# Attention with exponentials on two engines: the third shift of some VectorE tiles made by an accumulating transfer

## The chip, the cores and the metric

The kernel runs on one core of a Trainium2 chip. Times are device microseconds (us). The engines are TensorE (PE: matmuls, and PEld: its weight loads), VectorE (DVE), ScalarE (ACT), GpSimd (POOL) and SyncE (SP, which here only issues transfers). Each has its own queue of instructions and works through it in order. They meet through semaphores. Sixteen DMA engines move the data of every transfer.

## The reference

The program computes attention for 32 heads of 2048 queries and keys, with head size 20. Rows of q and k are scaled to length one, and a head has one factor t in place of the usual scale.

```python
qn = q / (jnp.sqrt((q * q).sum(axis=-1, keepdims=True)) + eps)
kn = k / (jnp.sqrt((k * k).sum(axis=-1, keepdims=True)) + eps)
logits = jnp.einsum('bhqd,bhkd->bhqk', qn, kn) * t[None, :, None, None]
attn = _softmax(logits, axis=-1)
return jnp.einsum('bhqk,bhkd->bhqd', attn, v)
```

All tensors are bf16. The dominant work is 32 x 2048 x 2048 exponentials.

## The kernel before, in words

**Tiles.** Keys lie on the 128 partitions, sixteen blocks of 128 (R = 16) in each head, and the 2048 queries in four groups of 512 columns. A tile is one block of keys by all queries: 128 x 2048 scores. The list `DVE_TILES` says how many of a head's sixteen tiles DVE works on; the others are ACT's, cut into units of 512 columns.

**ACT's tiles.** PE computes two or three units of scores into one of two halves of psA ("wave", line 758), ACT takes the exponential of all of them in one instruction into `p_ring` (line 849), and PE multiplies four units with V into psO (line 778). V has a column of ones, so that the same product sums the softmax's denominator.

**DVE's tiles.** PE computes scores into psD. DVE multiplies them and adds a constant, with an int16 result in a slot of `xt` (line 905, two conversions of 1024 columns to a tile, tasks `t1`). Read as fp16, that integer is a rough exponential. To flatten its error, the kernel averages four of them: the integer itself and three copies, shifted by 256, 512 and 768 (`PHASES`), each multiplied with V scaled by the matching power of two (`vph`, made on POOL, line 574). The shifts are integer additions from `xt` into `ss` (line 912 on DVE, tasks `s0`, `s1`, `s2`). The planner can give a shift to POOL instead, cut into pieces of 128 to 672 int32 words, each fitted into the time of a conversion on DVE (line 916). So a DVE tile costs two conversions, three shifts and four groups of products with V. There are `NX` = 6 slots of `xt` and `NE` = 4 of each `ss`.

**Preparation.** q, k and v are loaded by SP some three heads ahead (`LEAD`). DVE squares and sums, and computes the inverse root in a few small operations (tasks `rs`, lines 623 to 641); POOL folds the squares and normalizes (lines 612, 653). SP transposes, and copies q into a zero-padded layout `qz` and k into three rotated copies `kR`. Head 0 is prepared in its own way, with a scratch tensor `kx` that is not used later.

**End of a head.** When all products of a head are in psO, DVE transposes psO (task `tr`, line 791), which frees psO for the next head's products. DVE takes reciprocals, POOL divides (line 802), and SP stores.

**Order of the work.** All instructions are tasks with a planned duration, dependencies and a priority. `list_schedule` plays them out with these durations and so fixes each engine's order; `plan_waits` then sets the semaphore waits. The order is fixed before the program runs. An engine whose next instruction has to wait holds up all behind it. For a transfer, the plan has the duration of its issue (`dur`) and its time from then to landing (`lat`). `pool_fill` places POOL's pieces (tasks with `win`) into DVE's conversions; POOL's other tasks start when POOL is free. `schedule` repeats the play up to `PASSES` times, choosing for groups of score products between a light form and one that uses more of PE, so that PE's load in each 3.41 us stays above `LOAD`. `SWITCH`, `MARGIN`, `KEEP`, `SPARE`, `DSL`, `HOLDA` weigh its choices.

**Places that the change touches.** The constants of `Program` and of the kernel; `add_loads` (planned times of loads, and a gate by an earlier head's transpose); `add_prep` (the last `rs` operation); `add_dgroup` (the shifts and products of a DVE tile); `leave` in `list_schedule` and `plan_waits` (waits of POOL on itself).

Of the kernel before, what the change touches and what calls it, by code (L numbers as in the profile page):

```python
# [13 lines left out]
I16 = mybir.dt.int16  # L14
# [7 lines left out]
PHASES = (256, 512, 768)  # L22
# [23 lines left out]
class Program:  # L46
# [2 lines left out]

    SEM_LAT = {"PE": 0.20, "ACT": 0.30, "DVE": 0.14, "POOL": 0.15, "SP": 0.0}  # L50

    SWITCH = 0.1
    LIGHT = 9.0
    TICK = 3.41
    LOAD = 3550.0
    PASSES = 16
    FIRM = 8
    MARGIN = 600.0
    PE_REST = 4.2
    PV_SLACK = 0.6  # L60
    OVER = 0.03
    PRATE = 0.00164
    KEEP = 0.3
    RESTP = 0.3
    SPARE = 0.05
    DSL = 0.0
    HOLDA = 1.0
    HPE = 0.2
    HDV = 0.02
    HOLD = {"DVE": HDV, "PE": HPE}  # L70
# [74 lines left out]
    def list_schedule(self):  # L145
# [39 lines left out]
        def leave(t, now):  # L185

            for u in t.users:
                lat = t.lat if t.dma else (
                    self.SEM_LAT[t.eng] if u.eng != t.eng else 0.12 if t.eng == "DVE" else 0.0)
                if u.eng == "PE" and u.name[:2] == "pv":  # L190
                    lat += self.PV_SLACK
                rt[u.seq] = max(rt[u.seq], t.end + lat)
                u.n -= 1
                if u.n == 0:
                    arrive(u, max(now, rt[u.seq]))
# [138 lines left out]
    def plan_waits(self):  # L334
        pos = {}
        for e, ts in self.order.items():
            for i, t in enumerate(ts):
                pos[t.seq] = i
        for t in self.tasks:
            for d in t.deps:  # L340
                if not d.dma and (d.eng != t.eng or d.eng == "DVE" or t.name == "qt0"):
                    d.inc = True
        dma_cnt = {}
        for e, ts in self.order.items():
            c = 0
            for t in ts:
                if t.dma:
                    dma_cnt[t.dma] = dma_cnt.get(t.dma, 0) + 16
                    t.cnt = dma_cnt[t.dma]
                elif t.inc:  # L350
                    c += 1
                    t.cnt = c
        allt = sorted(self.tasks, key=lambda t: (t.start, pos[t.seq]))
        known = {e: {} for e in self.order}
        snap = {}
        waits = {}
        for t in allt:
            kn = known[t.eng]
            need = {}
            for d in t.deps:  # L360
                if not d.dma and d.eng == t.eng and d.eng != "DVE" and t.name != "qt0":
                    continue
                key = d.dma if d.dma else d.eng
                if need.get(key, (0, None))[0] < d.cnt:
                    need[key] = (d.cnt, d)
            ws = []
            for key, (c, d) in sorted(need.items(), key=lambda kv: -kv[1][1].end):
                if kn.get(key, 0) >= c:
                    continue
                ws.append((key, c))  # L370
                kn[key] = c
                for k2, c2 in snap[d.seq].items():
                    if kn.get(k2, 0) < c2:
                        kn[k2] = c2
            waits[t.seq] = ws
            snap[t.seq] = dict(kn)
        self.waits = waits
# [12 lines left out]
def bass_standalone__qk_norm__prompt_kernel(  # L390
# [16 lines left out]
    NB = 8  # L407
    NV = 6
    NN = 4
    NT = 3  # L410
    NX = 6
    NE = 4
    GD = 2
    GPN = (0, 0, 0, 0, 0, 0, 0, 0, 0, 0, 0, 0, 0, 0, 0, 0, 0, 0, 0, 0, 0, 0, 0, 0, 0, 0, 0, 0, 0, 0, 0, 0)
# [1 line left out]
    NWARM = 14  # L416
    EARLY = 3
    NSOLO = 3
    LEAD = 3.0
    SPREAD = 0.4  # L420
    FIRST = -7.0
    DLEAD = 0.75
    PE_MM = 0.23
    MORE = 12
    DLM = 2
    DVE_TILES = [4, 4, 4, 5, 4, 5, 5, 5, 5, 5, 5, 5, 5, 5, 6, 5, 6, 5, 5, 5, 5, 3, 5, 5, 5, 4, 5, 6, 6, 5, 5, 5]
    NDMAX = 6
    NPOOL, FPOOL = True, True
    FUSE, FOLD = True, 1
    NQ, NSQ, NSTEP = 2, 4, 0.0  # L430
    EXP0 = 0.051
    RSPOOL = False
    TTRATE = 0.00168
    TTDUR, TTWIN = 0.8, 0.55
    NCH = 1

    with ExitStack() as es:
# [18 lines left out]
        qz = [sbuf(f"qz{i}", [128, NG, 512], BF16) for i in range(NT)]  # L456
        kR = [sbuf(f"kR{i}", [128, 3, 512], BF16) for i in range(NT)]
        p_ring = sbuf("p_ring", [128, NP * 512], BF16)
        xt = [sbuf("xt", [128, NX * 2048], I16)]
        ss = [[sbuf(f"ss{j}", [128, NE * 2048], I16)] for j in range(len(PHASES))]  # L460
        oTs = [sbuf(f"oT{i}", [128, R, 32], F32) for i in range(2)]
# [10 lines left out]
        def dma(eng, name, dst, src, deps, pri, key, lat=2.2, dur=0.65):  # L472
            return add(eng, name, lambda e, tk: e.dma_start(dst, src), dur, deps, pri, lat=lat, dma=key)  # L473
# [77 lines left out]
        def add_loads(h):  # L551
            b, bv = (h + 1) % NB, h % NV
            pri = h - LEAD - 0.5
            war = (norm[h - NB] if h >= NB else []) + ([lambda: [trn[max(h - 3, 0) if h < 5 else h - 4]]] if h >= EARLY else [])
            x = qk_of(h)
            lds[h] = [dma("SP", f"ldk{h}", x[:, R:2 * R, :], k[0, h].rearrange("(p r) d -> p r d", p=128),
                          war, pri - 0.01 if h else -50, f"k{b}", lat=4.5 if h else 2.2)]
            if h == 0:
                lds[h].append(dma("ACT", "ldq0", x[:, 0:R, :], q[0, 0].rearrange("(p r) d -> p r d", p=128),
                                  [], -99, "q0a"))  # L560
            else:

                for nh in range(4):
                    src = bass.AP(q.tensor, q[0, h].offset + nh * D,
                                  [[16 * D, 32], [4 * D, 4], [512 * D, 4], [1, D]])
                    dst = x[32 * nh:32 * nh + 32, 0:R, :].rearrange("p (c g) d -> p c g d", g=4)
                    lds[h].append(dma("SP", f"ldq{h}", dst, src, war, pri, f"q{b}", lat=4.5))
            war = (pv_users[h - NV] if h >= NV else z_v[bv]) + ([lambda: [trn[h - 2]]] if h >= 2 else [])
            if h == 1:
                war = war + [lambda: [trn[0]]]  # L570
            ld_v[h] = dma("SP", f"ldv{h}", vaug[bv][:, :, 0:D], v[0, h].rearrange("(p r) d -> p r d", p=128),
                          war, pri + 0.1, f"v{bv}", lat=3.0)
            nd = 4 if h < DLM else DVE_TILES[h]
            vsc[h] = [add("POOL", f"vs{h}", lambda e, tk, i=i: e.tensor_scalar(  # L574
                vph[bv][:, i, 0:nd, :], vaug[bv][:, R - nd:R, :], 2.0 ** (-PHASES[i] / 1024.0), 1.0, ALU.mult, ALU.mult),
                0.4, [ld_v[h]] + (pv_users[h - NV] if h >= NV else z_v[bv]), pri + 0.2) for i in range(len(PHASES))]
            for u in vsc[h] if h else []:
                u.win = 0.14

        def add_prep(hs):  # L580
# [46 lines left out]
            def small(name, fn, deps):  # L627
                if RSPOOL and hs[0] > 2:
                    return pool(name, fn, 0.01 + 0.053 * 2 * n, deps)
                return dv(name, fn, 0.07 + 0.03 * n, deps)  # L630
# [7 lines left out]
            tq = t_f32[:, hs[0]:hs[0] + n]  # L638
            tq = bass.AP(tq.tensor, tq.offset, [tq.ap[0], [1, n], [0, R]])
            if hs[0]:  # L640
                c = small("rs", lambda e, tk: e.tensor_tensor(rq, rq, tq, ALU.mult), [c, tcp])
            if hs[0] == 0:
                first_head(c)
                prep_last[0] = norm[0] + head0[-1:]
# [223 lines left out]
        def place(r, n, m):  # L868
# [2 lines left out]
            head[r] += m  # L871
            return (head[r] - m) % n

        def add_dgroup(jg):
            js = D_groups[jg]
            sx = se = 0
            ox, oe = place(0, NX, len(js)), place(1, NE, len(js))
# [29 lines left out]
                        0.067 + W1 / 960.0, [qk] + old("x", i), due - 5)  # L907
                    t1s.append(t1_prev[nchunk[0]])
            sh = []
            for i in range(len(PHASES)):  # L910
                dst, w = ss[i][0], 2048 * len(js)
                f = add("DVE", f"s{i}.{js[0]}", lambda e, tk, i=i, dst=dst: e.tensor_scalar(  # L912
                    dst[:, be:be + w], xt[0][:, bx:bx + w], float(PHASES[i]), None, ALU.add), 0.068 + w / 3840.0,
                    t1s + [u for m in range(len(js)) for u in old(f"s{i}", m)], due)
                if len(js) == 1 and jg >= 2:
                    f.alt = lambda c, n, i=i, dst=dst: lambda e, tk: e.tensor_tensor(  # L916
                        dst[:, be + 2 * c:be + 2 * (c + n)].bitcast(I32), xt[0][:, bx + 2 * c:bx + 2 * (c + n)].bitcast(I32),
                        bass.AP(add_w, i, [add_w[:, :].ap[0], [0, n]]), ALU.add)
                sh.append([(list(range(len(js))), f)])
            for m in range(len(js)):  # L920
                new["x", ox + m] = [u for us in sh for ms, u in us if m in ms]
            for i, j in enumerate(js):
                h, rg = D_tiles[j]
                for nm, tile, dep, ph in [("x", xt[sx], t1s[2 * i:2 * i + 2], None)] + [
                        (f"s{n}", ss[n][se], [u for ms, u in sh[n] if i in ms], n) for n in range(len(PHASES))]:
                    p = add("PE", f"pv{nm}{j}", lambda e, tk, h=h, rg=rg, o=2048 * i + (bx if ph is None else be), tile=tile, ph=ph: pv_mm(
                        e, h, lambda g: rg[g],
                        lambda g: tile[:, o + 512 * GORD[g]:o + 512 * GORD[g] + 512].bitcast(FP16), ph),
                        PE_MM, dep + pv_base(h) + (vsc[h] if ph is not None else []), due + 0.2)
                    pv_users[h].append(p)  # L930
                    new.setdefault((nm, (ox if nm == "x" else oe) + i), []).append(p)
# [77 lines left out]
```

## Time and profile before

| What | Value |
|---|---|
| Time, median of 3 runs | 661.57 us (661.47 to 661.71) |
| The profiled execution: its own time, its span | 662.08 us, 660.4 us |
| ACT busy; its exponentials | 649.7 us; 568 in 642.5 us |
| DVE busy; conversions; shifts | 645.3 us; 314 in 381.9 us; 352 in 234.5 us |
| POOL busy; its pieces of shifts | 469.2 us; 335 in 322.5 us |
| PE busy | 591.1 us |
| Transfers | 36.25 MB, SP's queue took 34.9% of the 16 DMA engines' time |
| TensorE clock granted | 0.995 |

Busy time counts instructions from start to end, overlaps within an engine once. A group of instructions is given with its line, its engine, what it writes and reads, its count, then its busy time and mean duration, and the idle time of its engine just before it with what ended that. The chain that ended last is followed backward from the last instruction, at each step to what released it.

### The profile page before, as it was taken

What the parts mean: (1) busy time and instruction counts of PE and PEld (TensorE: products, weight loads), DVE (VectorE), ACT (ScalarE), POOL (GpSimd) and SP (SyncE); (2) the same over time, 40 slices, a digit from 0 to 9 for tenths busy, and PEclk for the clock granted to TensorE, in tenths of its full rate; (3) what the DMA queues carried; (4) which work ended last, traced back from release to release, by engine and by line L of the source; (5) the groups of instructions that cost most, each with busy time, mean ns of one, the idle gap of its engine ahead of it and who ended that gap; (6) DMA issues with size and microseconds to landing.
All of it is one profiled execution on the core that took longest, in us unless ns stands there. A gap on an engine that the chain in (4) does not pass through costs nothing.

```text
span 660.4 us, 14800 instructions
## 1 busy us (share of the span) xinstructions
PE 591.1 (90%) x5979; PEld 168.0 (25%) x6007; DVE 645.3 (98%) x902; ACT 649.7 (98%) x577; POOL 469.2 (71%) x542
## 2 busy tenths in 40 slices
PE   7887898888999888998989999899999889999997
PEld 2221222222222222222222222222222222222222
DVE  8998899999999999999999999999999999999997
ACT  9998899999999999999999999999999999999997
POOL 2675775678677877787777778787687865877652
PEclk9999899999999999999999999999999999999999
DMA  5544334343441524425235242452423424140200
GB/s 64 81 62 72 62 38 86 44 76 45 70 70 21 88 30 74 63 33 86 21 67 69 43 80 20 67 70 41 85 22 85 47 52 75 33 77 6 55 6 11
DMA packets 196724, 36.25 MB, mean 55 GB/s; under 512 B 172592, under 2 KB 196656, under 8 KB 196656
## 3 DMA queue, kind: packets, MB, share of 16 engines
q1 hardware_dynamic: 196512, 35.22, 34.9%
q8 instruction: 47, 0.77, 0.5%
q14 instruction: 21, 0.17, 0.1%
q10 hardware_dynamic: 144, 0.08, 0.1%
HBM read 7.87 MB, written 2.62 MB: 16 GB/s over the span
## 4 chain that ended last, share of the span: by engine, by line
ACT 81%; DVE 14%; PE 2%; SPq 1%; issue 1%; DMA 1%; POOL 0%; DVEq 0%
ACT p_ring L849 81%; DVE xt L905 7%; DVE ss L912 4%; SPq L473 1%; PE psO L685 1%; DMA kR<-qkT 1%; DVE rs_sum L619 1%; PE psO L778 1%; DVE sq L604 0%; DVE oT L791 0%; PE psD L758 0%; PE psA L758 0%; DVE qkn L660 0%; DVE qz L729 0%; DVE o_stage L802 0%
## 5 line engine op out<-in xcount | busy, mean ns | idle before, releaser
L849 ACT ACTIVATE p_ring<-psA 128x1024 bf16<-128x1024 f32 (+1 forms) x568 | 642.5, 1433 | 5.1 <-PE psA L758 5.0
L916 POOL TENSOR_TENSOR ss<-xt,add_w 128x672 int32<-128x672 int32 (+14 forms) x335 | 322.5, 969 | 110.5 <-DVE ss L912 58.0
L905 DVE TENSOR_SCALAR xt<-psD 128x1024 int16<-128x1024 f32 x314 | 381.9, 1216 | 9.2 <-PE psD L758 7.9
L758 PE MATMUL psA<-qz,kR 32*128 32x512 bf16 (+2 forms) x1048 | 218.6, 386 | 43.9 <-ACT p_ring L849 39.5
L912 DVE TENSOR_SCALAR ss<-xt 128x2048 int16<-128x2048 int16 x352 | 234.5, 681 | 0.3
L778 PE MATMUL psO<-ss,vph 128*32 128x512 f16 x1884 | 166.6, 386 | 0.0
L758 PE MATMUL psD<-qz,kR 64*128 64x512 bf16 (+1 forms) x466 | 121.0, 386 | 8.7 <-DVE xt L905 4.8
L758 PE MATMUL psA<-qz,qkT 32*128 32x512 bf16 (+2 forms) x350 | 115.8, 386 | 10.1 <-ACT p_ring L849 8.4
L778 PE MATMUL psO<-p_ring,vaug 128*32 128x512 bf16 x1420 | 124.3, 386 | 0.1
L758 PEld LDWEIGHTS psA<-qz,kR 32*128 32x128 bf16 (+2 forms) x1065 | 53.0, 92 | 180.9 <-ACT p_ring L849 179.7
L574 POOL TENSOR_SCALAR vph<-vaug 128x160 f16<-128x160 bf16 (+3 forms) x96 | 40.6, 423 | 32.5 <-DMA vaug<-in_v_dram 13.1
L778 PE MATMUL psO<-xt,vaug 128*32 128x512 f16 x628 | 62.4, 387 | 0.0
L778 PEld LDWEIGHTS psO<-ss,vph 128*32 128x32 f16 x1884 | 42.6, 94 | 69.8 <-issue 58.2
L758 PE MATMUL psD<-qz,qkT 64*128 64x512 bf16 (+1 forms) x156 | 59.1, 387 | 1.3 <-DVE xt L905 0.7
L653 POOL TENSOR_TENSOR qkn<-qk_sb,rs_r 128x640 bf16<-128x640 bf16 x29 | 47.6, 1641 | 14.3 <-DVE ss L912 5.0
L758 PEld LDWEIGHTS psD<-qz,kR 64*128 64x128 bf16 (+1 forms) x471 | 29.9, 93 | 71.3 <-DVE xt L905 44.3
L778 PEld LDWEIGHTS psO<-p_ring,vaug 128*32 128x32 bf16 x1420 | 32.6, 94 | 58.2 <-issue 48.9
L758 PEld LDWEIGHTS psA<-qz,qkT 32*128 32x128 bf16 (+2 forms) x355 | 27.9, 92 | 55.6 <-ACT p_ring L849 54.3
L802 POOL TENSOR_TENSOR o_stage<-oT,rec 128x320 bf16<-128x320 f32 x30 | 28.4, 946 | 14.7 <-DVE ss L912 7.1
L612 POOL TENSOR_TENSOR fold<-sq 128x320 f32<-128x320 bf16 x29 | 28.5, 982 | 9.4 <-DVE ss L912 5.8
L791 DVE STREAM_TRANSPOSE oT<-psO 128x512 f32<-128x512 f32 x32 | 22.6, 705 | 1.2 <-PE psO L778 1.0
L778 PEld LDWEIGHTS psO<-xt,vaug 128*32 128x32 bf16 x628 | 16.3, 94 | 28.1 <-issue 22.1
(48 smaller groups left out, 102.4 us busy)
## 6 DMA issues: line engine op xcount, KB each, us to landing
kR<-qkT SPq DMA_DIRECT2D x62, 96.0 KB, 2.1
qz<-qkT SPq DMA_DIRECT2D x124, 32.0 KB, 1.8
kR<-qkT SPq DMA_DIRECT2D x62, 64.0 KB, 2.0
qk_sb<-in_k_dram SPq DMA_DIRECT2D x32, 80.0 KB, 2.7
vaug<-in_v_dram SPq DMA_DIRECT2D x32, 80.0 KB, 3.6
qk_sb<-in_q_dram SPq DMA_DIRECT2D x124, 20.0 KB, 2.6
out_dram<-o_stage SPq DMA_DIRECT2D x31, 80.0 KB, 3.0
kR<-qkT SPq DMA_DIRECT2D x62, 32.0 KB, 1.9
```

The source lines that it names most:

```text
L473: return add(eng, name, lambda e, tk: e.dma_start(dst, src), dur, deps, pri, lat=lat, dma=key)
L574: vsc[h] = [add("POOL", f"vs{h}", lambda e, tk, i=i: e.tensor_scalar(vph[bv][:, i, 0:nd, :], vaug[bv][:, R - nd:R, :], 2.0 ** (-PHASES[i] ...
L612: c2.append(pool("fold", lambda e, tk, a=a, k=k, at=at: e.tensor_tensor(at[k + 1][0][:, a:a + 2 * R, :], at[k][0][:, a:a + 2 * R, 0:at[k + ...
L653: u = add("POOL", f"norm{h}", lambda e, tk, x=x, b=b, i=i, j=j: e.tensor_tensor(qkn[b][:, j:j + m, 0:D], x[:, j:j + m, :], bc(rs["r"][:, 2 ...
L758: return eng.matmul(dst, lhsT, mov, tile_position=(p0, 0))
L778: last = eng.matmul(psO[32 * g:32 * g + 32, :], w, rhs_of(g), start=start, stop=False, skip_group_check=True, tile_position=(0, 32 * g))
L791: trO[h] = add("DVE", f"tr{h}", lambda e, tk: e.transpose(oT[:, :, :].rearrange("p r d -> p (r d)"), psO[:, :]), 0.63, [lambda: pv_users[h ...
L802: fin[h] = add("POOL" if pool else "DVE", f"fin{h}", lambda e, tk: e.tensor_tensor(st, src, rb, ALU.mult), TTDUR if pool else 0.40, [rc] + ...
L849: act[w] = add("ACT", f"exp{w}", lambda e, tk: e.activation(p_ring[:, p0 * 512:p0 * 512 + n], psA[:, slot * WAVES[0] * 512:slot * WAVES[0] ...
L905: t1_prev[nchunk[0]] = add("DVE", f"t1.{j}.{k}", lambda e, tk, o=o, slot=slot: e.tensor_scalar(xt[sx][:, o:o + W1], psD[:, slot * W1:slot ...
L912: f = add("DVE", f"s{i}.{js[0]}", lambda e, tk, i=i, dst=dst: e.tensor_scalar(dst[:, be:be + w], xt[0][:, bx:bx + w], float(PHASES[i]), No ...
L916: f.alt = lambda c, n, i=i, dst=dst: lambda e, tk: e.tensor_tensor(dst[:, be + 2 * c:be + 2 * (c + n)].bitcast(I32), xt[0][:, bx + 2 * c:b ...
```

## The change

In 58 tiles of DVE, the third shift is no longer an instruction of DVE or POOL. The other two shifts are made as before. When these two and PE's product with the unshifted `xt` are done, POOL issues a transfer that adds a constant tensor of 768 (`cst`, which is `kx`, filled once by a memset on POOL after head 0's use of it) to the tile's `xt` slot in place. PE then multiplies the slot as the third shifted copy. `ACCN` lists how many tiles of a head are made so, spread over the head by `ASTEP`; the first four tiles and the last head have none. The slots of `xt` become eight. Each slot has its own semaphore for the transfer.

Besides, five more tiles go to DVE (162 in place of 157). The last `rs` multiplication goes to POOL from head 3 on (`RTPOOL`). POOL now waits by semaphore for its own earlier results. The loads get other planned durations, V's with an issue of 1.4 us and lower priority. The gate of head 5's loads (`LGATE`) and several of the planner's weights differ.

```diff
-    SWITCH = 0.1
+    SWITCH = 0.4
-    PASSES = 16
-    FIRM = 8
-    MARGIN = 600.0
+    PASSES = 20
+    FIRM = 10
+    MARGIN = 450.0
-    KEEP = 0.3
+    KEEP = 0.2
-    SPARE = 0.05
-    DSL = 0.0
-    HOLDA = 1.0
+    SPARE = 0.0
+    DSL = 0.5
+    HOLDA = 0.7
...
-                    self.SEM_LAT[t.eng] if u.eng != t.eng else 0.12 if t.eng == "DVE" else 0.0)
+                    self.SEM_LAT[t.eng] if u.eng != t.eng or t.eng == "POOL" else 0.12 if t.eng == "DVE" else 0.0)
...
-                if not d.dma and (d.eng != t.eng or d.eng == "DVE" or t.name == "qt0"):
+                if not d.dma and (d.eng != t.eng or d.eng in ("DVE", "POOL") or t.name == "qt0"):
...
-    NX = 6
+    NX = 8
-    LEAD = 3.0
+    LEAD = 3.1
-    DVE_TILES = [4, 4, 4, 5, 4, 5, 5, 5, 5, 5, 5, 5, 5, 5, 6, 5, 6, 5, 5, 5, 5, 3, 5, 5, 5, 4, 5, 6, 6, 5, 5, 5]
+    DVE_TILES = [4, 4, 5, 6, 4, 5, 5, 5, 5, 5, 6, 5, 5, 5, 6, 5, 5, 6, 5, 5, 5, 3, 5, 6, 5, 4, 5, 6, 6, 5, 6, 5]
+    RTPOOL = True
+    VPRI = 0.3
+    ACCN = (0, 2, 2, 2, 2, 2, 2, 1, 4, 2, 1, 2, 3, 2, 2, 2, 2, 2, 1, 2, 2, 0, 3, 2, 3, 0, 1, 4, 2, 2, 1, 5)
+    NLAST = 1
+    ASTEP, AOFF = 2, 0
+    ADUR, ALAT = 0.95, 8.0
+    ADUE = -0.3
+    LGATE = 1
...
+        cst = kx[:, :].bitcast(I16)
...
-            war = (norm[h - NB] if h >= NB else []) + ([lambda: [trn[max(h - 3, 0) if h < 5 else h - 4]]] if h >= EARLY else [])
+            war = (norm[h - NB] if h >= NB else []) + ([lambda: [trn[max(h - 3, 0) if h < 5 + LGATE else h - 4]]] if h >= EARLY else [])
...
-                          war, pri - 0.01 if h else -50, f"k{b}", lat=4.5 if h else 2.2)]
+                          war, pri - 0.01 if h else -50, f"k{b}", lat=4.5 if h else 2.2, dur=0.5)]
...
-                    lds[h].append(dma("SP", f"ldq{h}", dst, src, war, pri, f"q{b}", lat=4.5))
+                    lds[h].append(dma("SP", f"ldq{h}", dst, src, war, pri, f"q{b}", lat=4.5, dur=0.68))
...
-                          war, pri + 0.1, f"v{bv}", lat=3.0)
+                          war, pri + VPRI, f"v{bv}", lat=2.6, dur=1.4)
...
-                c = small("rs", lambda e, tk: e.tensor_tensor(rq, rq, tq, ALU.mult), [c, tcp])
+                f = lambda e, tk: e.tensor_tensor(rq, rq, tq, ALU.mult)
+                c = pool("rs", f, 0.02 + 0.027 * n, [c, tcp]) if RTPOOL and hs[0] > 2 else small("rs", f, [c, tcp])
...
+            if not z_cst:
+                z_cst.append(add("POOL", "z", lambda e, tk: e.memset(cst[:, :], PHASES[2]), 2.0, rot[0] + [trn[0]], -70))
...
-            for i in range(len(PHASES)):
+            h0, n0 = D_tiles[js[0]][0], js[0] - d0[D_tiles[js[0]][0]]
+            nd0 = DVE_TILES[h0]
+            kind = [(n * ASTEP + AOFF) % nd0 if math.gcd(ASTEP, nd0) == 1 else n for n in range(nd0)].index(n0)
+            by_dma = jg >= 4 and len(js) == 1 and h0 < H - NLAST and kind < ACCN[h0]
+            for i in range(len(PHASES) - by_dma):
...
+                uses = [("x", xt[sx], t1s[2 * i:2 * i + 2], None)] + [
+                    (f"s{n}", ss[n][se], [u for ms, u in sh[n] if i in ms], n) for n in range(len(sh))]
+                for nm, tile, dep, ph in uses + ([("y", xt[sx], None, 2)] if by_dma else []):
+                    if nm == "y":
+                        nm = "x"
+                        dep = [add("POOL", f"acc{j}", lambda e, tk: e.dma_start(xt[0][:, bx:bx + 2048], cst[:, :], accum_op=ALU.add),
+                                   ADUR, [u for us in sh for ms, u in us] + new["x", ox] + z_cst, due + ADUE, lat=ALAT, dma=f"A{ox}")]
```

More of the change, by code (lines that the diff above doesn't have):

```diff
@@ L360, in plan_waits @@
             for d in t.deps:
-                if not d.dma and d.eng == t.eng and d.eng != "DVE" and t.name != "qt0":
+                if not d.dma and d.eng == t.eng and d.eng not in ("DVE", "POOL") and t.name != "qt0":
                     continue
@@ L872, in place @@
             return (head[r] - m) % n
+        z_cst = []
         def add_dgroup(jg):
+            if not z_cst:
+                z_cst.append(add("POOL", "z", lambda e, tk: e.memset(cst[:, :], PHASES[2]), 2.0, rot[0] + [trn[0]], -70))
             js = D_groups[jg]
@@ L923, in add_dgroup @@
                 h, rg = D_tiles[j]
-                for nm, tile, dep, ph in [("x", xt[sx], t1s[2 * i:2 * i + 2], None)] + [
-                        (f"s{n}", ss[n][se], [u for ms, u in sh[n] if i in ms], n) for n in range(len(PHASES))]:
-                    p = add("PE", f"pv{nm}{j}", lambda e, tk, h=h, rg=rg, o=2048 * i + (bx if ph is None else be), tile=tile, ph=ph: pv_mm(
+                uses = [("x", xt[sx], t1s[2 * i:2 * i + 2], None)] + [
[5 more added lines that the diff above has]
+                                   ADUR, [u for us in sh for ms, u in us] + new["x", ox] + z_cst, due + ADUE, lat=ALAT, dma=f"A{ox}")]
+                    p = add("PE", f"pv{nm}{j}", lambda e, tk, h=h, rg=rg, o=2048 * i + (bx if nm == "x" else be), tile=tile, ph=ph: pv_mm(
                         e, h, lambda g: rg[g],
```

## The prediction

> **What bounds the kernel now.** I read the page's busy shares and groups first, then the chain that ended last, then the waits of ACT.
>
> ```profile
> span 660.4 us, 14800 instructions
> PE 591.1 (90%) x5979; PEld 168.0 (25%) x6007; DVE 645.3 (98%) x902; ACT 649.7 (98%) x577; POOL 469.2 (71%) x542
> ...
> ACT 81%; DVE 14%; PE 2%; SPq 1%; issue 1%; DMA 1%; POOL 0%; DVEq 0%
> ...
> L849 ACT ACTIVATE p_ring<-psA 128x1024 bf16<-128x1024 f32 (+1 forms) x568 | 642.5, 1433 | 5.1 <-PE psA L758 5.0
> L916 POOL TENSOR_TENSOR ss<-xt,add_w 128x672 int32<-128x672 int32 (+14 forms) x335 | 322.5, 969 | 110.5 <-DVE ss L912 58.0
> L905 DVE TENSOR_SCALAR xt<-psD 128x1024 int16<-128x1024 f32 x314 | 381.9, 1216 | 9.2 <-PE psD L758 7.9
> L912 DVE TENSOR_SCALAR ss<-xt 128x2048 int16<-128x2048 int16 x352 | 234.5, 681 | 0.3
> ```
>
> Two engines are full at once. ACT's exponentials fill 642.5 of 660.4 us with 5.1 us idle in front of them, and the chain is ACT for 81%. DVE is idle for only 15.1 us (660.4 - 645.3). So time falls only if both engines lose work.
>
> ```profile
> 60.72 3.97 DMA kR<-qkT
> ...
> 91.87 1.20 DVE ss L912 x2
> 93.08 1.13 DVE xt L905
> ...
> 123.63 532.56 ACT p_ring L849 x471
> ```
>
> These rows of the chain give pace, which is shorter than a mean duration because neighbours overlap. Two shifts take 1.20 us, so 0.60 each; a conversion takes 1.13; 471 exponentials take 532.56, so 1.131 each, and from 123.63 us on ACT never waits. Before that one wait, for the key copies of an early head, costs 3.97 us.
>
> ```profile
> ACT p_ring L849 <- PE psA L758: 5.0, 5, 2.8
> ```
>
> In the waits, ACT's only wait of weight is this one. It waits for PE: ACT has two halves of psA, and what covers a late PE is one exponential, about 1.13 us.
>
> **What the Trainium skill says.** "DMA: Bandwidth & Descriptors", section on SWDGE, HWDGE and iDMA: an accumulating DMA can only be issued from GpSimd, whose cores write its descriptors into rings in SBUF. No DMA of the kernel before is issued from POOL, so its trace doesn't show this. The same page, section on the anatomy of one DMA, prices a DMA at 2.0 us plus bytes over 436 GB/s; its rules say that an accumulate reads its destination and writes it later. "SBUF — State Buffer", section "Who interferes with whom": DVE and GpSimd share a port pair, whoever has it keeps it for the whole instruction, and the other blocks. The trace agrees, in its one collision of that kind:
>
> ```profile
> 120.18 1.37 DVE L912 TENSOR_SCALAR ss<-xt 128x2048 int16<-128x2048 int16 x1
> ...
> 120.07 0.93 POOL L916 TENSOR_TENSOR ss<-xt,add_w 128x416 int32<-128x416 int32 x1
> ```
>
> Rows of the two timelines around 120 us. POOL began 0.11 us before the shift; the shift took 1.37 us where the mean is 0.681. It sat out POOL's instruction and then ran. Everywhere else POOL's pieces lie inside conversions, which read PSUM.
>
> **The change, part by part.**
>
> ACT. The tile lists sum to 157 before and 162 after. Five tiles are 20 units of 512 columns less for ACT: 1420 to 1400 units, 568 to 560 exponentials, 8 x 1.131 = -9.05 us. If ACT stays as full, the span is 660.4 - 9.05 = 651.4 us.
>
> DVE. Five tiles add 10 conversions: 10 x 1.135 = +11.4 us. Shifts were 157 x 3 = 471, of which DVE's group shows 352, so POOL did 119. The rule with the list ACCN selects 58 tiles, so 162 x 3 - 58 = 428 remain. How many POOL keeps, no trace shows. If its share stays at 119, DVE has 309, 43 fewer: -25.8 us at 0.60. If each accumulate takes 0.95 us (the code's figure) from POOL's pieces, that is 55 us, and POOL spends 322.5 / 119 = 2.71 us a shift, so it loses 20: DVE has 329, 23 fewer, -13.8 us. I take POOL at 110, so 34 fewer, -20.4 us. The last small multiply of each preparation moves to POOL: thirteen of 176 ns and three of 165 ns, less some 80 ns of overlap each, -1.5 us; the normalization behind it starts one POOL instruction later, hidden by a lead of three heads, about 60 us. Sum: 11.4 - 20.4 - 1.5 = -10.5, so DVE is busy 634.8; with its 15.1 us idle kept, it could end at 649.9 (644.5 to 656.5 with the two ends). Just below ACT's 651.4.
>
> POOL. Added: 58 issues, 16 small multiplies, and one memset of the constant (planned at 2 us, early, behind head 0's copies). POOL is idle for 191 us. An issue's price is bounded below by SP's 0.6 us for a V load (median of its rows) and above by that plus a shift that it waits out, 1.3 us. 58 x 0.95 = 55 us fit its idle time, so nothing on the path as long as pieces and issues don't collide with DVE; if they do, see the second rival. The issue waits for the tile's two shifts and for PE's first use of xt. Behind that wait stand POOL's pieces, and behind them PE's products of those shifts.
>
> The transfer. A tile is 128 x 4096 B, 0.52 MB. By the skill's price a plain copy is 2.0 + 1.2 = 3.2 us; with the destination read too, 4.4 us, an estimate. The plan has PE wait for 8.0 us after the issue. With 35% of the DMA engines' time taken before, and 58 x 2.4 us = 139 us (21%) added, the sum of 56% leaves room; I expect 4 to 7 us. Behind the late product on PE stand the score products for ACT, so beyond the plan's 8 us plus some 1 us of cover each late microsecond is ACT's.
>
> PE. 20 more groups of four D products less 5 of A: 15 x about 0.22 us (two groups take 0.6 us at most in the timeline), 3.3 us, on an engine idle for 69. Hidden; if not, 3 us.
>
> Slots and loads. Eight xt slots hold 8 x 650 / 162 = 32 us of tiles; a tile that waits for its accumulate lives some 20 us (conversions 2.3, shifts 1.2, products and queue 5 or so, transfer 9). Six slots would hold 25. So no stall there. The loads keep number and size; only their planned issue times and priorities move, three heads ahead. V's issues are 0.6 us in the trace against 1.4 in the new plan, so V comes a little later than it need, behind a slack of heads: nothing. The early stall of 3.97 us may go or grow with the new leads: -4 to +4 us, taken as nothing.
>
> Sum: the later of ACT's 651.4 and DVE's 644.5, 649.9, 656.5, weighted one, two, one: 652.7 us of span. The profiled execution took 662.08, 1.7 us over its span, and 0.5 above the median 661.57. So span plus 1.2: 653.9, and I predict 654.
>
> **The rivals.** (1) ACT and DVE shrink as summed: 654, from 652.5 (ACT alone) to 658 (POOL loses most). Its own range is 648.5 to 659.
>
> (2) POOL's issues hold the port pair and shifts wait, as at 120 us. A conversion is DVE's work for 58% of the time. An issue of 0.95 us that starts anywhere in one overhangs it by 0.95 x 0.95 / 2 / 1.135 = 0.40 us on average, and a shift follows in some 6 of 10: 0.24; one that starts in a shift (a third of the time) waits, and takes the pair before another shift half the time: 0.16. So 0.40 us each, 58 x 0.40 = 23 us on an engine at 649.9: 673, plus 1.2 is 674.3. It decides from (660.4 - 649.9) / 58 = 0.18 us an issue: slower than that price, the kernel is slower than before. For it speaks the one collision; against it, that of an issue's time only a part need be writing, and no row shows which.
>
> (3) The accumulates land after PE wants them. From 9.05 / 58 = 0.16 us of ACT stall each, the gain is gone; at 1 us each the time is 652.5 + 58 = 710. Against it: 4 to 7 us expected against 8 planned.
>
> (4) It cancels: lockout near 0.18 us an issue, 661.6.
>
> **How the numbers follow.** Case 1 has 0.60 (with part of the lockout still faster), case 4 has 0.07, case 2 has 0.23, case 3 has 0.10. Within 0.2% is about what a measurement of this kernel can't tell from no change. Faster 0.60, same 0.07, slower 0.33. The range runs from 648.5 (ACT's bound with the early stall gone, 652.5 - 4) to 672: above it lie case 3's larger part and the upper half of case 2, some 0.13, below it 0.05.
>
> **What would show it.** Right: 560 exponentials with idle time before them under 8 us; DVE's shifts near 318 with a mean near 0.68 us; PE hardly waiting for an accumulate. Wrong by (2): shifts longer than 0.69 us in tens of rows, DVE busy above 650 us. Wrong by (3): PE's longest new wait is on the accumulating DMA, landings above 9 us, and ACT idle by tens of us. Wrong in the sum: POOL's pieces fall well below 300 us and DVE's shifts stay above 330.

## The result and the profile after

The changed kernel takes 682.63 us (679.99 to 685.74) against 661.53, the median of the kernel before with one more execution: 1.032 times the kernel before, 95% interval 1.0276 to 1.0365. It is slower by 21 us where 7.6 us less were forecast, and above the range that went to 672. The profiled execution took 683.26 us with a span of 681.5.

The page of the changed kernel; the groups have count, then busy us and mean ns, then idle time of the engine before them:

```profile
span 681.5 us, 14957 instructions
PE 602.8 (88%) x6046; PEld 168.9 (25%) x6067; DVE 649.1 (95%) x870; ACT 644.9 (95%) x569; POOL 467.5 (69%) x573
...
q1 hardware_dynamic: 196512, 35.22, 33.9%
q0 software_dynamic: 8352, 30.41, 24.5%
...
DVE 36%; ACT 36%; SPq 10%; PE 9%; DMA 5%; issue 2%; POOL 2%; DVEq 0%; POOLq 0%
...
L859 ACT ACTIVATE p_ring<-psA 128x1024 bf16<-128x1024 f32 (+1 forms) x560 | 637.7, 1345 | 28.7 <-PE psA L768 24.7
L919 DVE TENSOR_SCALAR xt<-psD 128x1024 int16<-128x1024 f32 x324 | 392.9, 1213 | 12.2 <-PE psD L768 12.0
L934 POOL TENSOR_TENSOR ss<-xt,add_w 128x672 int32<-128x672 int32 (+14 forms) x291 | 271.1, 941 | 76.9 <-DVE ss L930 39.5
L930 DVE TENSOR_SCALAR ss<-xt 128x2048 int16<-128x2048 int16 x326 | 227.2, 708 | 0.7
...
L947 POOL DMA_DIRECT2D xt<-kx x58 | 59.1, 1019 | 12.9 <-PE psO L788 7.9
```

The work has moved as the change says: 560 exponentials, 324 conversions, 326 shifts on DVE, 58 accumulates. But neither engine is full any more. ACT is idle for 36.6 us (681.5 - 644.9) where it was for 10.7, DVE for 32.4 where it was for 15.1. The chain, 81% ACT before, has SP's queue in it for 10% and DMA for 5%. The new queue q0, the accumulates, takes 24.5% of the sixteen DMA engines' time.

The waits of the changed kernel, us in total, times, longest:

```profile
POOL vph L583 <- DMA vaug<-in_v_dram: 47.6, 16, 6.5
...
ACT p_ring L859 <- PE psA L768: 24.7, 27, 4.5
...
PE psO L788 <- POOL ss L934: 8.5, 3, 4.3
```

In the kernel before, the first of these was:

```profile
POOL vph L574 <- DMA vaug<-in_v_dram: 13.1, 3, 10.0
```

So POOL waits 47.6 us for loads of V, 13.1 before, of which 10.0 were one wait at 8 to 18 us. PE waits for POOL's shifts, ACT for PE. No wait for an accumulate has any weight. One of these stalls in full, from the timelines of SP's queue and of POOL:

```profile
599.97 5.84 SPq L482 DMA_DIRECT2D kR<-qkT  x6
605.86 4.61 SPq L482 DMA_DIRECT2D qz<-qkT  x4
610.51 3.77 SPq L482 DMA_DIRECT2D kR<-qkT  x6
614.33 0.61 SPq L482 DMA_DIRECT2D vaug<-in_v_dram  x1
```

```profile
599.59 0.87 POOL L947 DMA_DIRECT2D xt<-kx  x1 [0.59 <-PE psO L788]
...
601.31 1.18 POOL L947 DMA_DIRECT2D xt<-kx  x1 [0.31 <-PE psO L788]
...
617.76 1.12 POOL L583 TENSOR_SCALAR vph<-vaug 128x160 f16<-128x160 bf16 x3 [6.54 <-DMA vaug<-in_v_dram]
618.96 2.25 POOL L934 TENSOR_TENSOR ss<-xt,add_w 128x480 int32<-128x480 int32 x2
```

Two accumulates were issued at 599.6 and 601.3. SP's six copies took 5.84 us to issue and the next four 4.61; the later six, with the engines less loaded, took 3.77. V's load stood behind all sixteen and landed at about 617.6. POOL stood at the scaling of V for 6.54 us, with a piece of a shift behind it that PE needed: the chain goes from that piece to PE's products at 620.00. The same stretch by windows (busy us of PE, PEld, DVE, ACT, POOL, each with its count; then the granted clock, the DMA engines' share, GB/s):

```profile
602.00:604.00 2.00, 1.91 (x27) 0.49 (x23) 2.00 (x3) 2.00 (x3) 1.70 (x3) 1.00 1.06 200
606.00:608.00 2.00, 2.00 (x29) 0.68 (x27) 2.00 (x3) 2.00 (x3) 0.78 (x2) 1.00 0.99 197
...
616.00:618.00 2.00, 0.00 (x0) 0.00 (x0) 0.77 (x1) 0.71 (x1) 0.24 (x1) 1.00 0.72 76
618.00:620.00 2.00, 0.00 (x1) 0.00 (x2) 0.00 (x0) 0.00 (x0) 1.76 (x5) 0.54 0.00 0
620.00:622.00 2.00, 1.70 (x9) 0.45 (x11) 0.98 (x2) 0.80 (x1) 1.21 (x1) 0.50 0.00 0
```

The DMA engines are full at 602 to 608, 8 to 14 us before PE, DVE and ACT stop. And the stop has a tail: PE stood idle, its clock was granted at 0.50 to 0.54 and it started again at half speed. Over the whole run the clock was 0.974, 0.995 before.

### The profile page after: what moved, and what is told of

The parts are those of the page before. It is cut to its first block, busy times and chain, and to the rows that moved or that the text cites. A ratio compares the mean times of both kernels' runs of the same rounds, so it can differ in the third digit from the quotient of the medians.

```text
span 681.5 us, 14957 instructions
## 1 busy us (share of the span) xinstructions
PE 602.8 (88%) x6046; PEld 168.9 (25%) x6067; DVE 649.1 (95%) x870; ACT 644.9 (95%) x569; POOL 467.5 (69%) x573
## 3 DMA queue, kind: packets, MB, share of 16 engines
q1 hardware_dynamic: 196512, 35.22, 33.9%
q0 software_dynamic: 8352, 30.41, 24.5%
## 4 chain that ended last, share of the span: by engine, by line
DVE 36%; ACT 36%; SPq 10%; PE 9%; DMA 5%; issue 2%; POOL 2%; DVEq 0%; POOLq 0%
ACT p_ring L859 36%; DVE xt L919 20%; DVE ss L930 11%; SPq L482 9%; PE psO L788 3%; PE psA L768 3%; DMA vaug<-in_v_dram 2%; PE psD L768 2%; DVE oT L801 1%; DMA kR<-qkT 1%; DVE rs_sum L628 1%; DMA qkT<-qkn 1%; DVE sq L613 1%; PE psO L695 1%; POOL ss L934 1%
## 5 line engine op out<-in xcount | busy, mean ns | idle before, releaser
L919 DVE TENSOR_SCALAR xt<-psD 128x1024 int16<-128x1024 f32 x324 | 392.9, 1213 | 12.2 <-PE psD L768 12.0
L934 POOL TENSOR_TENSOR ss<-xt,add_w 128x672 int32<-128x672 int32 (+14 forms) x291 | 271.1, 941 | 76.9 <-DVE ss L930 39.5
L930 DVE TENSOR_SCALAR ss<-xt 128x2048 int16<-128x2048 int16 x326 | 227.2, 708 | 0.7
L788 PE MATMUL psO<-ss,vph 128*32 128x512 f16 x1712 | 158.0, 389 | 9.0 <-POOL ss L934 8.5
L768 PE MATMUL psD<-qz,kR 64*128 64x512 bf16 x485 | 126.4, 391 | 27.4 <-DVE xt L919 21.4
L583 POOL TENSOR_SCALAR vph<-vaug 128x160 f16<-128x160 bf16 (+3 forms) x96 | 40.0, 417 | 62.1 <-DMA vaug<-in_v_dram 47.6
L947 POOL DMA_DIRECT2D xt<-kx x58 | 59.1, 1019 | 12.9 <-PE psO L788 7.9
L768 PE MATMUL psD<-qz,qkT 64*128 64x512 bf16 (+1 forms) x162 | 62.6, 395 | 3.0 <-DVE xt L919 2.0
L768 PEld LDWEIGHTS psD<-qz,kR 64*128 64x128 bf16 x486 | 30.5, 93 | 103.5 <-DVE xt L919 87.8
L768 PEld LDWEIGHTS psA<-qz,qkT 64*128 64x128 bf16 (+2 forms) x350 | 27.5, 92 | 53.2 <-ACT p_ring L859 47.6
L621 POOL TENSOR_TENSOR fold<-sq 128x320 f32<-128x320 bf16 x29 | 25.9, 893 | 19.8 <-DVE ss L930 14.1
```

The source lines that it names most:

```text
L768: return eng.matmul(dst, lhsT, mov, tile_position=(p0, 0))
L788: last = eng.matmul(psO[32 * g:32 * g + 32, :], w, rhs_of(g), start=start, stop=False, skip_group_check=True, tile_position=(0, 32 * g))
L919: t1_prev[nchunk[0]] = add("DVE", f"t1.{j}.{k}", lambda e, tk, o=o, slot=slot: e.tensor_scalar(xt[sx][:, o:o + W1], psD[:, slot * W1:slot ...
L947: dep = [add("POOL", f"acc{j}", lambda e, tk: e.dma_start(xt[0][:, bx:bx + 2048], cst[:, :], accum_op=ALU.add), ADUR, [u for us in sh for ...
```

## The experiments

The theory T after this profile: the bytes of the accumulates fill the DMA engines; SP's issues and landings come late; V is late, POOL stands, and what is behind it holds up PE and then ACT and DVE. Rival P: the new plan puts V's load too late in any case. Rival L: POOL's issues and pieces hold the port pair that DVE's shifts need.

**1. The accumulates cut to 64 columns.** The third shift of the other columns of these tiles is not computed.

```diff
-e.dma_start(xt[0][:, bx:bx + 2048], cst[:, :], accum_op=ALU.add)
+e.dma_start(xt[0][:, bx:bx + 64], cst[:, 0:64], accum_op=ALU.add)
```

> The changed kernel with each of the 58 accumulating transfers cut from 2048 to 64 columns (4096 to 128 B a partition); the third shift of the other columns of these tiles is left out. Every engine's instructions, their order and their waits stay as they are. Theory T (the bytes of the accumulates fill the DMA engines, SP's issues take longer, V lands late, POOL stands at the scaling of V, and its late pieces hold up PE and DVE): SP's issues fall from 465 to about 410 us in sum, POOL waits for V for under 20 us instead of 47.6, ACT idles for under 20 us instead of 36, time 652 to 662. Rival P (the new plan's order puts V's load too late whatever the traffic): 675 or more, POOL's wait for V still over 35 us. Rival L (POOL's issues and pieces hold the port pair that DVE's shifts need): 675 or more, since the 58 issues stay.

Measured: 650.75 us, 0.9837 (0.9821 to 0.9854) of the kernel before. Its page:

```profile
span 648.5 us, 14978 instructions
PE 593.7 (92%) x6067; PEld 168.1 (26%) x6067; DVE 641.1 (99%) x870; ACT 640.7 (99%) x569; POOL 470.6 (73%) x573
...
q0 software_dynamic: 8352, 0.95, 3.1%
...
L859 ACT ACTIVATE p_ring<-psA 128x1024 bf16<-128x1024 f32 (+1 forms) x560 | 633.5, 1401 | 0.4 <-PE psA L768 0.2
...
L947 POOL DMA_DIRECT2D xt<-kx x58 | 56.7, 977 | 14.5 <-PE psO L788 9.2
```

This is 1.25 us below T's range. All 32 us between this and the changed kernel come from the transfers' bytes: the orders on all engines are the same, and the 58 issues on POOL still take 0.98 us each. P and L fall as main causes. SP's issues, summed over the trace, take 409 us here, 465 in the changed kernel and 407 in the kernel before. POOL's wait for V is 5.7 us, ACT idles for 7.8.

**2. Half, three quarters, a plain copy, shorter packets.** Four runs that again leave all orders as they are. With 1024 and 1536 columns, the third shift of the other columns is left out. In the plain copy, the constant overwrites the slot and the third term is not computed. In the last, each row goes in two pieces of 2048 B, and all is computed.

```diff
-e.dma_start(xt[0][:, bx:bx + 2048], cst[:, :], accum_op=ALU.add)
+e.dma_start(xt[0][:, bx:bx + 1024], cst[:, 0:1024], accum_op=ALU.add)   # half
+e.dma_start(xt[0][:, bx:bx + 1536], cst[:, 0:1536], accum_op=ALU.add)   # three quarters
+e.dma_start(xt[0][:, bx:bx + 2048], cst[:, :])                          # plain copy
+e.dma_start(xt[0][:, bx:bx + 2048].rearrange("p (a b) -> p a b", a=2),  # two pieces a row
+            bass.AP(kx, 0, [kx[:, :].ap[0], [0, 2], [1, 1024]]).bitcast(I16), accum_op=ALU.add)
```

> The changed kernel with the accumulating transfers cut to half, 1024 of 2048 columns; the third shift of the other half of these tiles is left out. All orders stay. If the loss grows in proportion to the bytes: halfway between the small transfers' 650.75 and 682.6, so 664 to 669. If it sets in when several transfers fill the engines for longer than the plan's slack: 651 to 658.

> The changed kernel with the accumulating transfers cut to 1536 of 2048 columns; the third shift of the last quarter is left out. All orders stay. Measured so far: 64 columns 650.75, 1024 columns 652.1, 2048 columns 682.6. If the loss sets in when the plan's slack is used up: between 655 and 670, far from a straight line between 1024 and 2048 only if the knee lies sharp. If it were in proportion to bytes over the whole range, 1024 columns would have shown 667 already.

> The changed kernel with plain copies of the same size in place of accumulating ones: the constant overwrites the slot, so the third term of these tiles is not computed. All orders stay, as many bytes are written, but the destination isn't read first. If reading the destination makes the transfer dear: the queue's share falls from 24.5% to about 12 to 15%, time 652 to 664. If accumulating costs nothing beside the copy: share near 24%, time 675 to 690.

> The changed kernel with each accumulate described as two pieces of 2048 B a partition in place of one of 4096 B (the constant's first half read twice, the result the same). All orders stay. If long accumulating packets are what holds up the small packets of the other queue: time falls below 672. If the engines' total time counts: the queue's share stays at 24.5% or above, time 678 to 690. A longer issue on POOL (0.92 us before) is a side effect that can only slow it.

The accumulates' queue in each, in this order:

```profile
q0 software_dynamic: 8352, 15.21, 14.2%
```

```profile
q0 software_dynamic: 8352, 22.81, 19.2%
```

```profile
q0 software_dynamic: 8352, 30.41, 12.6%
```

```profile
q0 software_dynamic: 15776, 30.41, 26.7%
```

| Transfer | Engine time of one (share x span / 58) | POOL's wait for V | Time | Ratio to before (95%) |
|---|---|---|---|---|
| 64 columns, added | 0.35 us | 5.7 us | 650.75 us | 0.9837 (0.9821 to 0.9854) |
| 2048 columns, copied | 1.41 us | 10.2 us | 652.55 us | 0.9874 (0.9842 to 0.9906) |
| 1024 columns, added | 1.59 us | 12.3 us | 652.09 us | 0.9869 (0.9838 to 0.9900) |
| 1536 columns, added | 2.21 us | 27.7 us | 665.56 us | 1.0066 (1.0047 to 1.0086) |
| 2048 columns, added | 2.88 us | 47.6 us | 682.63 us | 1.0320 (1.0276 to 1.0365) |
| 2048 columns, added in two pieces | 3.15 us | 26.9 us | 687.85 us | 1.0408 (1.0365 to 1.0451) |

The same tile costs 1.41 us as a copy and 2.88 us as an accumulate, and the time follows the engines' time, not the bytes written. Up to 1.6 us a transfer it hardly matters; from there to 2.9 us each further 0.65 us costs 13 to 17 us of the kernel. So the loss is no price per transfer or per byte: it sets in late, and POOL's wait for V grows along with it. That it sets in where the load takes up the slack of the fixed order, as the half transfers' expectation put it second, fits these rows, but that slack was not measured by itself.

The last row shows no gain from shorter packets, but it doesn't settle their part. Its issues on POOL are longer, 1.22 us in the median where they were 0.92, the side effect that its expectation named. DVE's shifts are at 737 ns in the mean (708 in the changed kernel) and DVE is busy for 660.3 us (649.1). So its last 5 us may be these issues and the pieces behind them, and a gain could be hidden under them.

**3. The other constants alone.** No accumulates, and the tile list of before.

```diff
-    DVE_TILES = [4, 4, 5, 6, 4, 5, 5, 5, 5, 5, 6, ...
+    DVE_TILES = [4, 4, 4, 5, 4, 5, 5, 5, 5, 5, 5, ...   # the list of before, 157 tiles
-    ACCN = (0, 2, 2, 2, 2, 2, 2, 1, 4, ...
+    ACCN = (0,) * 32
```

> The changed kernel without any accumulate and with the tile list of the kernel before (157 tiles); all other new constants stay (eight xt slots, V's planned loads, the planner's weights, the last rs multiply on POOL). T and L: 658 to 665, the kernel before within half a per cent. P: 668 or more, with POOL's wait for V over 35 us.

Measured: 659.29 us, 0.9965 (0.9951 to 0.9979) of before. The new plan by itself is no loss but gains 0.35%, and POOL's wait for V is 7.4 us, so P falls here too. Among the kernels that compute everything this is the fastest.

**4. V's loads planned as before.**

```diff
-    VPRI = 0.3
+    VPRI = 0.1
...
-                          war, pri + VPRI, f"v{bv}", lat=2.6, dur=1.4)
+                          war, pri + VPRI, f"v{bv}", lat=3.0)
```

> The changed kernel with V's loads planned as in the kernel before (0.1 in priority, issue 0.65, landing 3.0 us); the planner makes a new order from that. T: the transfers are still there, POOL still waits for V by tens of us, time 670 to 695. P: POOL's wait for V goes back to about 13 us, time 652 to 664. L: 675 or more with POOL's wait for V of any size.

Measured: 711.98 us, 1.0741 (1.069 to 1.0791). That is above the ranges of T and P; only L's open range (675 or more) takes it in, and experiment 1 speaks against L. POOL's wait for V is 45.4 us, and DVE waits 18.4 us for q, up to 7.6 at a time. The planner's order differs on every engine, so this shows only that the old plan of V does not cure the loss.

**5. The scalings of V later in POOL's queue.** POOL's order alone is changed.

```diff
         prog.schedule()
+        ts = prog.order["POOL"]
+        for t in [t for t in ts if t.name[:2] == "vs" and int(t.name[2:]) > 4]:
+            to = min(t.start + VLATE, min(u.start for u in t.users) - 4.0)
+            i = ts.index(t)
+            j = i
+            while j + 1 < len(ts) and ts[j + 1].start <= to:
+                j += 1
...
```

> The changed kernel with only POOL's queue reordered: from head 5 on, the three scalings of V of each head stand some 6 us of planned time later in POOL's queue, behind pieces that they stood ahead of. Transfers, SP's order and all other engines' orders stay. T: POOL's wait for V falls from 47.6 to about 15 us, what stood behind it is on time, time 660 to 670. P: the same fall, so this run doesn't part T from P. L: 678 or more. If the accumulates' own traffic hurts by another way than V (late q, k or their copies), time stays above 672 though POOL's wait for V is gone.

Measured: 680.75 us, 1.0286 (1.0255 to 1.0317). POOL's wait for V did fall, to 3.2 us, and DVE's idle time from 32.4 to 20.4. But shifts on DVE met POOL's instructions more often; that the moved scalings no longer fit into conversions and made the pieces behind them late is argued from the order. Shifts that lasted 0.72 us or more went from 39 to 46, their mean from 708 to 740 ns:

```profile
PE 604.8 (89%) x6067; PEld 167.9 (25%) x6067; DVE 659.0 (97%) x870; ACT 646.2 (95%) x569; POOL 468.9 (69%) x573
```

DVE is busy 9.9 us longer than in the changed kernel: what the wait gave, the longer shifts took. The time lies where L had it, and also where the expectation put a loss by another way than V. The run removed one wait and made another, and decides nothing between them.

**6. V's load earlier in SP's queue.** SP's order alone is changed; POOL's stays.

```diff
         prog.schedule()
+        ts = prog.order["SP"]
+        for t in [t for t in ts if t.name[:3] == "ldv" and int(t.name[3:]) > 4]:
+            to = max([t.start - VEARLY] + [d.end + (d.lat if d.dma else 0.3) for d in t.deps])
+            i = j = ts.index(t)
+            while ts[j - 1].start >= to:
+                j -= 1
...
```

> The changed kernel with only SP's queue reordered: from head 5 on, V's load stands ahead of the 10 to 18 copies of q and k layouts that it stood behind (at most 12 us of planned time earlier, never before what it waits for). All 58 full transfers stay, and POOL's, DVE's, ACT's and PE's orders stay, so no piece of POOL's leaves its place as in the run with the scalings moved. If late V on POOL is the main channel of the loss: POOL's wait for V falls from 47.6 us to under 15, DVE's longer shifts go with it, time 655 to 670. If transfers late in another way (q, k, the copies that are now each one slot later, the accumulates before PE's products) cost as much: 670 to 685.

Measured: 673.78 us (670.99 to 676.33), 1.0224 (1.0179 to 1.027) of before, some 9 us less than the changed kernel. Waits for transfers that are left:

```profile
DVE sq L613 <- DMA qk_sb<-in_q_dram: 4.3, 2, 3.3
...
PE psD L768 <- DMA kR<-qkT: 3.9, 1, 3.9
POOL vph L583 <- DMA vaug<-in_v_dram: 3.1, 1, 3.1
```

DVE is busy for 641.1 us, as in experiment 1, and its long shifts are down to 20 (23 there). So late V costs about 9 of the 32 us, lockouts (shifts of DVE that wait out an instruction of POOL) included. This is a net figure, since the copies behind V now come a slot later. In the changed kernel's trace, four of PE's stops (at 71, 326, 533 and 616 us, 15.9 us in all) stand beside POOL's four longest waits for V.

About 23 us are left, in the second expectation's range. In this profile ACT is idle for 26.1 us (7.8 in experiment 1), and 13.9 of them lie at three stops. The one at 108 us ends with a late landing of key copies, the one at 205 us with a late q. The largest is at 471 us, where SP's six key copies took 6.44 us to issue and PE then stood for 5.6 us; that PE waited there for these copies is argued from the order, since the profile names no releaser. The rest is small gaps and was not traced.

```profile
108.67 3.28 DMA kR<-qkT
```

```profile
466.87 6.44 SPq L482 DMA_DIRECT2D kR<-qkT  x6
```

**7. More slack in the plan.** V's landing planned at 8.0 us; then all landings and issues longer.

```diff
-                          war, pri + VPRI, f"v{bv}", lat=2.6, dur=1.4)
+                          war, pri + VPRI, f"v{bv}", lat=8.0, dur=1.4)
...
# and in the second kernel besides: q and k lat=9.0 with dur=0.78 and 0.6; transposes lat=4.5, dur=1.5;
# copies and stores lat=3.5, dur=0.75
```

> The changed kernel with V's landing planned at 8.0 us after its issue in place of 2.6; the planner makes a new order in which the scalings of V fit DVE's conversions again. All 58 full transfers stay. If V's lateness on POOL is the main channel (V): POOL's wait for V under 10 us, time 655 to 668. If late V is only one of several transfers whose lateness costs (M): POOL's wait for V goes, DVE's and PE's waits for q and for the key copies stay or grow, time 668 to 682.

> The changed kernel with every load and copy planned as on busy DMA engines: landings of V 8.0, q and k 9.0, transposes 4.5, copies and stores 3.5 us; issues some 15% longer. All 58 full transfers stay. V: no better than with V's landing alone, 655 to 668. M: clearly better than with V alone, waits of all engines for transfers under 10 us in sum, time 653 to 665. If a plan's slack can't help because SP's issues themselves run late (S): above 675.

Measured: 683.4 us, 1.035 (1.0282 to 1.0418), and 678.72 us, 1.0269 (1.0236 to 1.0302). The first shows the waits of M (6.9 us of POOL for V, 7.7 of DVE for q) and lies 1.4 us above M's range. In the second, the waits for V and q are nearly gone (2.4 us for V, none for q), and PE's two waits for key copies are 1.6 us at most. But its time is hardly better, and lies in the range of S. Whether S is the reason is open. The order that the planner made with these latencies is another one: POOL gets fewer shifts to do (226 pieces, 291 in the changed kernel), and DVE more.

```profile
L930 DVE TENSOR_SCALAR ss<-xt 128x2048 int16<-128x2048 int16 x343 | 231.8, 687 | 1.5
```

How much of the loss is this order and how much the transfers, no run shows; neither order was run with small transfers.

**8. Fewer accumulates.** 28 of them, 159 tiles on DVE, V's landing at 3.2 us, and a set of weights for that list.

```diff
-    ACCN = (0, 2, 2, 2, 2, 2, 2, 1, 4, 2, 1, 2, 3, ...
+    ACCN = (0, 1, 1, 1, 1, 1, 0, 1, 2, 0, 1, 1, 1, ...
...
-    DVE_TILES = [4, 4, 5, 6, ...
+    DVE_TILES = [4, 4, 4, 5, ...
```

> A version with fewer accumulates: 28 full ones, about one a head, tile list of 159, landings of V planned at 3.2 us, and the planner's weights SWITCH 0.3, KEEP 0.3, DSL 0, HOLDA 1.3, LEAD 3.2, SPREAD 0.5, VPRI 0.1, ADUE -0.1. If the accumulates' time on the DMA engines is the cause, their share falls to about 12%, as with half transfers, and the time is 652 to 659, below the kernel before. If any full accumulate costs by itself: 666 or more.

Measured: 663.82 us, 1.0034 (1.0016 to 1.0052). The queue's share is 12.2%, as expected, but the time is 5 us above the range. ACT is idle for 15.2 us, 5.2 of them at 63 to 70 us, where the kernel before stalls too (4.6 us). So a share that cost nothing in the order of experiment 2 is no warrant for another order; this order was not run with small transfers either. No version with accumulates that computes everything beat the kernel before.

## Why the prediction was wrong

**ACT.** Right. 560 exponentials were forecast, and ACT busy at 649.7 - 9.05 = 640.7 us; with small transfers it is 640.7.

**DVE.** About right. 634.8 us were forecast; with small transfers it is 641.1. The difference is shifts, 326 where 318 were taken (8 x 0.60 = 4.8 us), and some lockouts. The kept idle time of 15.1 us was too much: the early stall went, and with small transfers DVE is idle for 7.4 us of a span of 648.5. That the sum still came out near, 649.9 for DVE, is luck: the two errors cancel.

**POOL's issue.** Right in size: 0.92 us in the median, inside 0.6 to 1.3. Rival 2, which put 0.40 us on each, is wrong in mechanism; the last section shows it. Its sign was there all the same: 65 shifts of the changed kernel took over 0.69 us, and DVE was busy for 649.1 us where 650 was the mark. But of the 42 that took over 0.70 us, 35 met another instruction of POOL. The seven that met an issue alone lost 0.5 us in all.

**The transfer: the step that failed.** The prediction added up 35% and 21% of engine time and held that "the sum of 56% leaves room". Its size was not far off: 33.9% and 24.5% measured, 2.88 us for one where 2.4 was estimated; landing 5.4 us in the median, 4 to 7 expected. (The plain copy of experiment 2 landed after 3.8 us, where the prediction had 3.2.) What failed was to take a mean share for room. Each accumulate keeps the engines for 3.2 us in the median, and where two to four came together the trace shows 6 to 12 us without a break. What comes in that time on SP's queue is late: in the changed kernel, ten loads of k issued while an accumulate was under way took 1.8 us on average to issue, the other 22 took 0.64. What the runs show in place of "room" is a loss of 32 us, all of it gone when the same transfers move 64 columns.

**Slots and loads: "nothing" was wrong.** The prediction had written that V "comes a little later than it need, behind a slack of heads". V's slack is in heads for PE's products, but not for POOL: POOL's scaling of V stands in a fixed order at V's planned landing, and everything on POOL's queue behind it waits. That price, named nowhere in the working, is 47.6 us of POOL's time and, net, about 9 us of the kernel's. The other 23 us are only in part traced to single transfers.

**Rival 3** had the right kind of thing, a late transfer that stalls PE's queue in front of ACT, but the wrong transfer. The accumulates came in time for PE; they made the others late. Of its signs, ACT's idle time came and PE's wait for an accumulate did not. Its threshold held: ACT's idle time grew by 25.9 us, to 36.6, more than the 9.05 that it gained.

The sum therefore was near for a chip with free DMA engines (654 predicted, 650.75 measured) and lacked one term of 32 us.

## What to carry to other kernels

Work moved to a resource that is idle on average is not free when what already runs there stands in a fixed order with exact landing times: here the DMA engines were idle for nearly two thirds of the time before, and the kernel still lost 32 us to their load. Look at what the DMA engines do in windows of the length of one transfer, not at their mean share, and list for each queue which engine stands at whose landing and what is queued behind it. The quickest test is to keep every instruction and shrink only the bytes.

## What was not expected of the hardware

Adding into SBUF cost the DMA engines twice what a copy did here: a packet of 4096 B takes 357 ns with the addition and 175 ns without (means of the 7424 packets in the traces), and a transfer landed after 5.4 us in place of 3.8 (medians). The issue on POOL is dearer, too, 0.92 us in place of 0.75 in the median.

POOL's issue of such a transfer mostly did not keep DVE out, unlike its compute instructions. From the timelines of DVE and of POOL in the changed kernel:

```profile
103.36 0.68 DVE L930 TENSOR_SCALAR ss<-xt 128x2048 int16<-128x2048 int16 x1
```

```profile
103.20 0.97 POOL L947 DMA_DIRECT2D xt<-kx  x1
```

The shift began 0.16 us into the issue and took its usual 0.68 us. The issue was a little longer than its shortest, 0.86. Of the 41 shifts that began inside an issue with at least 0.1 us of it left, 29 took 0.70 us or less (median of all 41: 0.683). The rule of the Trainium skill that one of the two blocks for the whole instruction ("SBUF — State Buffer", "Who interferes with whom") holds for POOL's pieces here, as the shift of 1.37 us before showed. For the issue of an accumulate as a whole it doesn't, and the measurement decides.
